# Attention decode backward on one core: two bf16 row tiles transposed as one fp32 block

## The chip, the cores and the metric

The kernel runs on one core of a Trainium2 chip. Its engines are TensorE (PE, with weight loads shown apart as PEld), VectorE (DVE), ScalarE (ACT), GpSimd (POOL) and SyncE (SP); the last two issue the DMA transfers here. The time is device microseconds of one launch. The median of three runs before the change is 1280.13 us (1279.72 to 1282.18).

## What is computed

Attention with one query row per head, forward and backward, for 64 heads (2 x 32), 8192 keys and a head size of 128, all bf16:

```python
scale = q.shape[-1] ** -0.5
scores = jnp.einsum("bhqd,bhkd->bhqk", q, k) * scale
p = _softmax(scores, axis=-1)
return jnp.einsum("bhqk,bhkd->bhqd", p, v)
```

The outputs are this result and the gradients of q, k and v for a given `grad_out`. Per head, with P the softmax row: dP = grad_out . v for every key, dS = P * (dP - sum(P * dP)), dq = scale * sum(dS * k), dk = scale * dS x q and dv = P x grad_out. K and V are read once and dK and dV are written once: 2 MB each per head, 268 MB in and 268 MB out.

## The kernel before

**Tiles.** A head's K is one tile kvt of 128 partitions x 64 rows x 128 (8192 keys, 64 on each partition), its V another. Twelve such tiles stay on chip, six heads of K and V. Later, dV is written over V and dK over K in the same tile, which is stored from there; the next load into a tile has to wait until that store has landed. Loads are issued by SyncE (L100), stores by GpSimd (L445, L89); the last head's stores go in pieces by SyncE.

**Chunks.** A tile is worked on in 4 chunks of 16 row blocks. The loop near the end counts steps g, 8 per head: in steps 0 to 3 the chunks of K are transposed, in steps 4 to 7 those of V. Everything else for a head follows at fixed steps after that, so in one step the work of up to four heads stands side by side. The order on each engine is written out by hand: every instruction of the loop goes through `pin`, which keeps program order.

**Scores.** `transpose_chunk` (L194, L196) turns 16 blocks of 128 keys x 128 into PSUM with 16 transposes, kvt as weights and a bf16 identity as the moving operand, into the tile tp (two buffers), and ScalarE copies the 128 x 2048 result to ev (two buffers). One step later `score_chunk` (L208) makes scores from it: four matmuls, each with 32 weight columns taken from qdT and 512 moving columns of ev, each into its own 32 partitions of PSUM (its own column group of the array). Among the 32 weight columns only one is not zero: qdT holds each head's q (or grad_out) column with zeros around it, so that a window shifted by the chunk's number puts the result into the chunk's own row. Over 4 chunks the tile raw collects 4 x 4 useful rows of 512. `keep_raw` (L221, VectorE) copies raw to rows, and `spread_rows` (L228) brings them back with four fp32 matmuls against a small selection matrix sel4, so that scores (or dP) stand as 128 partitions x 64.

**Softmax.** Step 5: maximum per partition on VectorE (L240). Step 6: maximum over partitions through an fp32 transpose (L244) and a reduction (L246). Step 7: spread to all partitions (L251), negated (L261), exponential on ScalarE (L271), which stands in ScalarE's queue behind the copy of step 7, then the bf16 weights E_pad (L280). Later: sums through a matmul with ones (L315), reciprocal (L324), the same for dS (L286, L338, L349, L358).

**Sums over keys.** `acc` (L372) multiplies kvt by E_pad or dS_pad, four matmuls per chunk in two column groups; `pick` (L389, L395, VectorE) and `join` (L409) reduce the result to one column. **Outer products.** `outer` (L427, VectorE) overwrites a chunk of kvt; it needs q or grad_out on all partitions, which `broadcast` (L178, L187) makes with a matmul against the identity.

**Around the change.** On TensorE, a step's order is: broadcast (steps 4 and 6), 16 transposes, joins, acc, spread_rows, max_spread, then the scores of the chunk transposed one step before. On VectorE: outer first, then the copies, maxima and sums of the step. On ScalarE: the copy of the step, in step 7 the exponential behind it. `begin` gives a head one PSUM tile sw that holds both score arrays, the broadcast and the small results. At the start q and grad_out land in qd_nat (partly by GpSimd's queue), two transposes (L154) and two copies (L155) make qdT of all heads.

Of the kernel before, what the change touches and what calls it, by code (L numbers as in the profile page):

```python
# [9 lines left out]
ALU = mybir.AluOpType  # L10
AX = mybir.AxisListType
BF16 = mybir.dt.bfloat16
F32 = mybir.dt.float32

CH = 16
QT = 4
CW = 64
NG = 2
SG = 4
SW = 32  # L20
# [6 lines left out]
def kernel(  # L27
# [11 lines left out]
    nc = tc.nc  # L39
    B, H, Sq, D = q.shape  # L40
    Sk = k.shape[2]
    P = nc.NUM_PARTITIONS
    assert Sq == 1 and D == P
    BH = B * H
# [3 lines left out]
    NCH = NT // CH  # L48
    SL = 2 * NCH
    scale = float(D) ** -0.5  # L50
# [3 lines left out]
    pin = tc.keep_in_program_order  # L54
# [65 lines left out]
        load(j, 0)  # L120
        load(j, 1)

    ident_bf = const.tile([P, P], BF16)
    masks.make_identity(nc, ident_bf[:])
    ident_f = const.tile([P, P], F32)
    masks.make_identity(nc, ident_f[:])
    ones = const.tile([P, 1], F32)
    nc.vector.memset(ones[:], 1.0)
    groups = [g * P // NG for g in range(NG)]
# [8 lines left out]
    nc.vector.memset(E_pad[:], 0.0)  # L138
    nc.vector.memset(dS_pad[:], 0.0)

    sel4 = const.tile([P, NCH, SG], F32)
    nc.vector.memset(sel4[:], 0.0)
    for g in range(SG):
        nc.vector.tensor_copy(
            out=sel4[g * SW : (g + 1) * SW, :, g],
            in_=ident_f[g * SW : (g + 1) * SW, g * SW : g * SW + NCH],
        )

    Q0 = NCH - 1
    qdT = const.tile([P, 2, Q0 + NCH * BH + SW], BF16)  # L150
    nc.vector.memset(qdT[:], 0.0)
    for w in range(2):
        tps = ps_m.tile([P, BH], BF16, tag=f"acc{w}", name="tps")
        nc.tensor.transpose(tps[:], qd_nat[:BH, w, :], ident_bf[:BH, :BH])  # L154
        nc.vector.tensor_copy(  # L155
            out=qdT[:, w, Q0 : Q0 + NCH * BH].rearrange("p (i f) -> p i f", f=NCH)[:, :, 0],
            in_=tps[:],
        )

    dqT = const.tile([P, BH], BF16)  # L160
    oT = const.tile([P, BH], BF16)
# [1 line left out]
    def begin(i):  # L163
# [7 lines left out]
        h.lsum = sw[:, 2 * NT + 2 * P : 2 * NT + 2 * P + 2]  # L171
        h.mb = sw[:, 2 * NT + 2 * P + 2 : 2 * NT + 2 * P + 3]

    def broadcast(i, w):

        h = heads[i]
        pin(
            nc.tensor.matmul(  # L178
                h.qbp,
                lhsT=qdT[:, w, Q0 + NCH * i : Q0 + NCH * i + 1].to_broadcast([P, P]),  # L180
                rhs=ident_bf[:],
                start=True,
                stop=True,
            )
        )
        h.qb[w] = small.tile([P, D], BF16, tag=f"qb{w}", name="qb")
        pin(nc.vector.tensor_copy(out=h.qb[w][:], in_=h.qbp))  # L187

    def transpose_chunk(i, c):
        w, c = divmod(c, NCH)  # L190
        src = heads[i].tile[w]
        tp = ps_tp.tile([P, CH, P], BF16, tag="tp", name="tp")
        for t in range(CH):
            pin(nc.tensor.transpose(tp[:, t, :], src[:, c * CH + t, :], ident_bf[:]))  # L194
        ev = evp.tile([P, CH, P], BF16, tag="ev", name="ev")
        pin(nc.scalar.copy(out=ev[:], in_=tp[:]))  # L196
        return ev

    def score_chunk(i, c, ev):

        h = heads[i]
        w, c = divmod(c, NCH)
        if c == 0:
            h.raw = ps_sdp.tile([P, QT * P], F32, tag="raw", name="raw")
        q0 = Q0 + NCH * i - c
        for g in range(SG):
            pin(
                nc.tensor.matmul(  # L208
                    h.raw[g * SW : (g + 1) * SW, :],
                    lhsT=qdT[:, w, q0 : q0 + SW],  # L210
                    rhs=ev[:, g * QT : (g + 1) * QT, :].rearrange("p n d -> p (n d)"),
                    start=(c == 0),
                    stop=(c == NCH - 1),
                )
            )
# [7 lines left out]
    def spread_rows(i, w):  # L223

        h = heads[i]
        for t in range(QT):
            pin(
                nc.tensor.matmul(  # L228
                    h.score[w].rearrange("p (n t) -> p n t", t=QT)[:, :, t],
                    lhsT=h.rows[:, t * P : (t + 1) * P],  # L230
                    rhs=sel4[:].rearrange("p c g -> p (c g)"),
                    start=True,
                    stop=True,
                )
            )

    def max_part(i):
        h = heads[i]
        h.mp = small.tile([P, 1], F32, tag="mp", name="mp")
        pin(nc.vector.reduce_max(out=h.mp[:], in_=h.s, axis=AX.X))  # L240

    def max_all(i):
        h = heads[i]
        pin(nc.tensor.transpose(h.mT, h.mp[:], ident_f[:]))  # L244
        h.gm = small.tile([1, 1], F32, tag="gm", name="gm")
        pin(nc.vector.reduce_max(out=h.gm[:], in_=h.mT, axis=AX.X))  # L246

    def max_spread(i):
        h = heads[i]
        pin(  # L250
            nc.tensor.matmul(  # L251
                h.mb,
                lhsT=ones[0:1, :].to_broadcast([1, P]),
                rhs=h.gm[:],
                start=True,
                stop=True,
            )
        )
        h.negm = small.tile([P, 1], F32, tag="negm", name="negm")
        pin(  # L260
            nc.vector.tensor_scalar(  # L261
                out=h.negm[:], in0=h.mb, scalar1=-scale, scalar2=None, op0=ALU.mult
            )
        )

    def expo(i):
        h = heads[i]
        h.E_f = work.tile([P, NT], F32, tag="E_f", name="E_f")
        h.ld = small.tile([P, 2], F32, tag="ld", name="ld")
        pin(  # L270
            nc.scalar.activation(  # L271
                out=h.E_f[:],
                in_=h.s,
                func=ACT.Exp,
                bias=h.negm[:],
                scale=scale,
                accum_out=h.ld[:, 0:1],
            )
        )
        pin(nc.vector.tensor_copy(out=E_pad[:, 0:NT], in_=h.E_f[:]))  # L280
# [39 lines left out]
    def normalise_p(i):  # L320
        h = heads[i]
        total(h.lsum[:, 0:1], h.ld[:, 0:1])
        h.rl = small.tile([P, 1], F32, tag="rl", name="rl")
        pin(nc.vector.reciprocal(out=h.rl[:], in_=h.lsum[:, 0:1]))  # L324
        pairs(i, 1, h.E_f, h.rl[:], "p2")
        h.rls = small.tile([P, 1], F32, tag="rls", name="rls")
        pin(
            nc.vector.tensor_scalar(
                out=h.rls[:], in0=h.rl[:], scalar1=scale, scalar2=None, op0=ALU.mult
            )  # L330
        )

    def normalise_ds(i):
        h = heads[i]
        total(h.lsum[:, 1:2], h.ld[:, 1:2])
        negdelta = small.tile([P, 1], F32, tag="negdelta", name="negdelta")
        pin(
            nc.vector.tensor_scalar(  # L338
                out=negdelta[:],
                in0=h.lsum[:, 1:2],  # L340
                scalar1=h.rl[:],
                scalar2=-1.0,
                op0=ALU.mult,
                op1=ALU.mult,
            )
        )
        dSu = work.tile([P, NT], F32, tag="dSu", name="dSu")
        pin(
            nc.vector.scalar_tensor_tensor(  # L349
                out=dSu[:],  # L350
                in0=h.dp,
                scalar=negdelta[:],
                in1=h.E_f[:],
                op0=ALU.add,
                op1=ALU.mult,
            )
        )
        pin(nc.vector.tensor_copy(out=dS_pad[:, 0:NT], in_=dSu[:]))  # L358
        pairs(i, 0, dSu, h.rls[:], "ds2")

    def acc(i, w, c):

# [42 lines left out]
    def join(i, w):  # L405

        h = heads[i]
        pin(
            nc.tensor.matmul(h.acc[w][:, 0:1], lhsT=h.sel[:], rhs=ones[:], start=True, stop=True)  # L409
        )  # L410
        pin(
            nc.vector.tensor_scalar(
                out=(oT if w else dqT)[:, i : i + 1],
                in0=h.acc[w][:, 0:1],
                scalar1=(h.rl if w else h.rls)[:],
                scalar2=None,
                op0=ALU.mult,
            )
        )
# [32 lines left out]
    last = list(range(1, NCH + 1))  # L452
    AHEAD = NTILE // 2

    prev = None
    for g in range(SL * BH + O0 + NCH + 4 - SL):
        now = [(g // SL - b, g % SL + b * SL) for b in range(4)]
# [2 lines left out]
        def at(r0):  # L460

            return next((i for i, r in now if r == r0), None)
# [37 lines left out]
        if prev is not None:  # L500
            score_chunk(*prev)
        prev = (g // SL, g % SL, ev) if ev is not None else None

        if (i := at(NCH)) is not None:
            keep_raw(i)
# [16 lines left out]

    for w, (src, dst) in enumerate(((dqT, out_1), (oT, out_0))):
        tps = ps_m.tile([BH, P], BF16, tag=f"acc{w}", name="tps")
        nc.tensor.transpose(tps[:], src[:], ident_bf[:])
        nat = evp.tile([P, CH, P], BF16, tag="ev", name="nat")
        nc.vector.tensor_copy(out=nat[:BH, 0, :], in_=tps[:])
        load_eng.dma_start(out=dst.rearrange("b h s d -> (b h s) d"), in_=nat[:BH, 0, :])
# [30 lines left out]
```

## Time and profile before

| | |
|---|---|
| median of the runs | 1280.13 us |
| profiled execution, span | 1280.2 us |
| ev copies, ScalarE, L196 | 512 x 1865 ns = 954.5 us |
| outer products, VectorE, L427 | 512 x 1216 ns = 616.8 us |
| transposes, TensorE, L194 | 8192 x 220 ns, 544.4 us busy |
| scores, TensorE, L208 | 2048 x 391 ns, 205.2 us busy |
| acc, TensorE, L372 | 2048 x 393 ns, 320 us busy |
| spread_rows weight loads, fp32, L228 | 1024 x 192 ns, 124.7 us busy |
| loads and stores | 537 MB, 421 GB/s over the span |

Busy time is the time in which at least one instruction of the row is under way. TensorE instructions are pipelined, so 8192 transposes of 220 ns each make 544 us, not 1802; what one costs in a stream is read from the distance between starts. An idle time with "<-" names what ended it. "issue" is time for which the profile shows no wait. In the chain of waits each piece is the work that the next one waited for, followed back from the end.

### The profile page before, as it was taken

How to read it: one execution, taken by the hardware profiler on the slowest of the kernel's cores; microseconds unless marked ns; L12 is line 12 of the kernel's file. 1: busy time of each engine (PE TensorE's matmuls, PEld its weight loads, DVE VectorE, ACT ScalarE, POOL GpSimd, SP SyncE). 2: the span in 40 equal slices, each digit the busy share in tenths (PEclk: the TensorE clock that was granted, in tenths of full speed). 3: DMA queues.
4: the chain of work that ended last, by engine and by line, in shares of the span. 5: the costliest groups of instructions: out<-in, count | busy, mean ns of one | idle time of the engine just before them, and what ended most of it. 6: DMA issues, size and time to landing. Idle time of an engine off the chain costs nothing.

```text
span 1280.2 us, 32473 instructions
## 1 busy us (share of the span) xinstructions
PE 1190.2 (93%) x14148; PEld 810.6 (63%) x14148; DVE 1025.8 (80%) x2256; ACT 975.3 (76%) x641; POOL 76.0 (6%) x143
## 2 busy tenths in 40 slices
PE   6999999999999999999999999999999999999994
PEld 5666666666666666666666666666666666666662
DVE  2888887888877888888888878788778888888885
ACT  6777777778777777777777777787777777777771
POOL 0000000000000000000000000000000000000000
PEclk9999999999999999999999999999999999999996
DMA  9999999999999999999999999999999999999996
GB/s 392 423 428 428 428 427 429 430 426 429 427 430 425 414 427 429 428 423 428 428 429 419 425 428 426 427 421 427 427 423 421 427 429 428 420 425 428 428 411 273
DMA packets 40155, 539.03 MB, mean 421 GB/s; under 512 B 5196, under 2 KB 5196, under 8 KB 6476
## 3 DMA queue, kind: packets, MB, share of 16 engines
q1 hardware_dynamic: 20172, 272.70, 50.1%
q0 software_dynamic: 19840, 264.25, 49.0%
q8 instruction: 110, 1.80, 0.5%
q14 instruction: 33, 0.27, 0.1%
HBM read 268.47 MB, written 268.47 MB: 419 GB/s over the span
## 4 chain that ended last, share of the span: by engine, by line
PE 59%; DVE 16%; ACT 10%; issue 10%; DMA 4%; POOL 0%; SPq 0%; ACTq 0%; POOLq 0%; DVEq 0%
PE tp L194 24%; PE acc L372 15%; ACT ev L196 9%; PE raw L208 9%; DVE kvt L427 6%; PE sw L228 4%; DVE sel L395 4%; DMA out_dram<-kvt 3%; DVE rows L221 3%; PE sw L315 3%; PE sw L178 2%; PE acc L409 2%; ACT E_f L271 1%; DVE sel L389 1%; DVE E_pad L280 1%
## 5 line engine op out<-in xcount | busy, mean ns | idle before, releaser
L196 ACT COPY ev<-tp 128x2048 bf16<-128x2048 bf16 x512 | 954.5, 1865 | 275.6 <-PE tp L194 268.9
L427 DVE TENSOR_TENSOR kvt<-qb,pair 128x2048 bf16<-128x2048 bf16 x512 | 616.8, 1216 | 0.2
L194 PE MATMUL tp<-ident_bf,kvt 128*128 128x128 bf16 x8192 | 544.4, 220 | 0.0
L194 PEld LDWEIGHTS <-kvt 128*128 128x128 bf16 x8192 | 482.4, 99 | 81.6 <-issue 80.7
L208 PE MATMUL raw<-ev,qdT 128*32 128x512 bf16 x2048 | 205.2, 391 | 1.5 <-ACT ev L196 1.5
L372 PE MATMUL acc<-kvt,E_pad 128*64 128x512 bf16 x1024 | 160.2, 393 | 24.5 <-DVE E_pad L280 24.5
L372 PE MATMUL acc<-kvt,dS_pad 128*64 128x512 bf16 x1024 | 159.8, 393 | 0.1
L228 PEld LDWEIGHTS sw<-sel,rows 128*128 128x128 f32 x1024 | 124.7, 192 | 52.4 <-DVE sel L395 25.9
L395 DVE SCALAR_TENSOR_TENSOR sel<-acc,diag,sel 128x128 f32<-128x128 f32 x384 | 134.8, 351 | 13.6
L208 PEld LDWEIGHTS <-qdT 128*32 128x32 bf16 x2048 | 53.1, 93 | 136.6 <-issue 131.8
L228 PE MATMUL sw<-sel,rows 128*128 128x16 f32 x1024 | 137.1, 266 | 0.0
L445 POOL DMA_DIRECT2D out_dram<-kvt x118 | 63.3, 536 | 1094.0 <-DVE kvt L427 555.7
L221 DVE COPY rows<-raw 128x512 f32<-128x512 f32 x128 | 88.6, 692 | 22.4 <-PE raw L208 22.4
L280 DVE CAST E_pad<-E_f 128x64 bf16<-128x64 f32 x64 | 12.5, 195 | 80.3 <-ACT E_f L271 80.3
L372 PEld LDWEIGHTS <-E_pad 128*64 128x64 bf16 x1024 | 36.1, 108 | 49.9 <-DVE E_pad L280 35.7
L178 PE MATMUL sw<-ident_bf,qdT 128*128 128x128 bf16 x128 | 28.5, 223 | 38.2 <-DVE mp L240 38.2
L246 DVE TENSOR_REDUCE gm<-sw 1x1 f32<-1x128 f32 x64 | 17.9, 279 | 55.4 <-PE sw L244 55.4
L315 PEld LDWEIGHTS sw<-ld,ones 128*128 128x128 f32 x256 | 38.1, 188 | 29.7 <-issue 15.0
L372 PEld LDWEIGHTS <-dS_pad 128*64 128x64 bf16 x1024 | 36.4, 108 | 22.3 <-DVE dS_pad L358 1.0
L315 PE MATMUL sw<-ld,ones 128*128 128x1 f32 x256 | 49.1, 261 | 0.0
L409 PE MATMUL acc<-ones,sel 128*128 128x1 f32 x256 | 43.3, 239 | 5.3 <-DVE sel L395 5.3
L389 DVE TENSOR_SCALAR sel<-acc,diag 128x128 f32<-128x128 f32 x128 | 43.8, 342 | 0.0
(49 smaller groups left out, 377.1 us busy)
## 6 DMA issues: line engine op xcount, KB each, us to landing
out_dram<-kvt POOLq DMA_DIRECT2D x118, 2048.0 KB, 40.6
kvt<-in_v_dram SPq DMA_DIRECT2D x64, 2048.0 KB, 19.1
kvt<-in_k_dram SPq DMA_DIRECT2D x63, 2048.0 KB, 19.4
out_dram<-kvt POOLq DMA_DIRECT2D x8, 2016.0 KB, 44.9
out_dram<-kvt SPq DMA_DIRECT2D x8, 512.0 KB, 10.9
kvt<-in_k_dram SPq DMA_DIRECT2D x2, 512.0 KB, 4.3
kvt<-in_k_dram SPq DMA_DIRECT2D x1, 1024.0 KB, 6.9
out_dram<-kvt POOLq DMA_DIRECT2D x8, 32.0 KB, 44.3
```

The costliest lines, as they stand in the source:

```text
L194: pin(nc.tensor.transpose(tp[:, t, :], src[:, c * CH + t, :], ident_bf[:]))
L196: pin(nc.scalar.copy(out=ev[:], in_=tp[:]))
L208: nc.tensor.matmul(h.raw[g * SW : (g + 1) * SW, :], lhsT=qdT[:, w, q0 : q0 + SW], rhs=ev[:, g * QT : (g + 1) * QT, :].rearrange("p n d -> ...
L221: pin(nc.vector.tensor_copy(out=h.rows[:], in_=h.raw[:]))
L228: nc.tensor.matmul(h.score[w].rearrange("p (n t) -> p n t", t=QT)[:, :, t], lhsT=h.rows[:, t * P : (t + 1) * P], rhs=sel4[:].rearrange("p ...
L315: nc.tensor.matmul(out, lhsT=ones[:].to_broadcast([P, P]), rhs=col, start=True, stop=True)
L372: nc.tensor.matmul(h.acc[w][g : g + CW, :], lhsT=wts[:, n0 : n0 + CW], rhs=rows[:, n0 : n0 + QT, :].rearrange("p n d -> p (n d)"), start=( ...
L389: nc.vector.tensor_scalar(out=h.sel[:], in0=block, scalar1=diag[:, 0:1], scalar2=None, op0=ALU.mult)
L395: nc.vector.scalar_tensor_tensor(out=h.sel[:], in0=block, scalar=diag[:, b : b + 1], in1=h.sel[:], op0=ALU.mult, op1=ALU.add,)
L409: nc.tensor.matmul(h.acc[w][:, 0:1], lhsT=h.sel[:], rhs=ones[:], start=True, stop=True)
L427: nc.vector.tensor_tensor(out=h.tile[w][:, n0 : n0 + CH, :].rearrange("p n (e t) -> p n e t", t=2), in0=h.qb[w][:] .rearrange("p (e t) -> ...
L445: pin(eng.dma_start(out=dst[:, b0:b1, :], in_=h.tile[w][:, b0:b1, :]))
```

## The change

Two neighbouring row blocks of kvt, 128 partitions x 256 bf16, are read as 128 x 128 fp32, each fp32 being the pair (d = 2j, d = 2j + 1) of one key row. One fp32 transpose with an fp32 identity turns them. After it, partition p holds pair j = p mod 64 of row block p div 64, and along the free side stand the 128 key partitions, each as two bf16: even d and odd d. A chunk takes 8 transposes for 16. tp and ev become 128 x 1024 fp32, as many bytes as before.

The scores are then two sums, one over even and one over odd d. `score_chunk` still makes four matmuls with 32 weight columns and 512 moving columns, but they are now (half of the chunk) x (even, odd): the moving operand is every second bf16 of ev, and the weights have two non-zero columns, one for the upper 64 partitions and one for the lower. `spread_rows` adds even and odd up, with a selection matrix that sums two column groups. The weights are no longer windows into an array of all heads: a small array qwin has zeros around two columns, and ScalarE copies a head's two columns into it (`window`), once for K and once for V. At the start there are more small transposes and copies to make q and grad_out in even and odd form (qpair), beside the plain form (qT) for the broadcast. The bf16 identity is now the upper half of the fp32 identity's elements, read with a stride. Eight one-column tiles of the softmax become columns of one tile st.

The core of the diff:

```diff
+    ident_bf = ident_f[:].bitcast(BF16).rearrange("p (n e) -> p n e", e=2)[:, :, 1]
...
+    sel4 = const.tile([P, NCH, SG // 2, 2], F32)
...
+    Q0 = 2 * NCH - 2
+    qT = const.tile([P, 2, BH], BF16)
+    qpair = const.tile([P, 2, BH, 2, 2], BF16)
+    nc.vector.memset(qpair[:], 0.0)
+    qwin = const.tile([P, 2, 2, Q0 + SW], BF16)
+    nc.vector.memset(qwin[:], 0.0)
+    qd_pair = evp.tile([P, 2, 2, 2, D // 2], BF16, tag="ev", name="qd_pair")
+    for w in range(2):
+        nc.vector.tensor_copy(
+            out=qd_pair[:BH, w],
+            in_=qd_nat[:BH, w, :]
+            .rearrange("p (j e) -> p e j", e=2)
+            .unsqueeze(2)
+            .to_broadcast([BH, 2, 2, D // 2]),
+        )
+        for e in range(2):
+            tps = ps_m.tile([P, BH], BF16, tag=f"acc{e}", name="tps")
+            nc.tensor.transpose(
+                tps[:],
+                qd_pair[:BH, w, e].rearrange("p t j -> p (t j)"),
+                ident_bf[:BH, :BH],
+            )
+            for t in range(2):
+                half = slice(t * D // 2, (t + 1) * D // 2)
+                nc.vector.tensor_copy(out=qpair[half, w, :, e, t], in_=tps[half, :])
...
+    def window(i, w):
+
+        pin(nc.scalar.copy(out=qwin[:, w, :, Q0 : Q0 + 2], in_=qpair[:, w, i]))
+
...
-        tp = ps_tp.tile([P, CH, P], BF16, tag="tp", name="tp")
-        for t in range(CH):
-            pin(nc.tensor.transpose(tp[:, t, :], src[:, c * CH + t, :], ident_bf[:]))
-        ev = evp.tile([P, CH, P], BF16, tag="ev", name="ev")
+        tp = ps_tp.tile([P, CH // 2, P], F32, tag="tp", name="tp")
+        for m in range(CH // 2):
+            n0 = c * CH + 2 * m
+            two = src[:, n0 : n0 + 2, :].rearrange("p n d -> p (n d)").bitcast(F32)
+            pin(nc.tensor.transpose(tp[:, m, :], two, ident_f[:]))
+        ev = evp.tile([P, CH // 2, P], F32, tag="ev", name="ev")
         pin(nc.scalar.copy(out=ev[:], in_=tp[:]))
...
+        q0 = Q0 - 2 * c
+        cols = (
+            ev[:]
+            .rearrange("p m s -> p (m s)")
+            .bitcast(BF16)
+            .rearrange("p (b s e) -> p b s e", b=SG // 2, e=2)
+        )
         for g in range(SG):
+            b, e = divmod(g, 2)
             pin(
                 nc.tensor.matmul(
                     h.raw[g * SW : (g + 1) * SW, :],
-                    lhsT=qdT[:, w, q0 : q0 + SW],
-                    rhs=ev[:, g * QT : (g + 1) * QT, :].rearrange("p n d -> p (n d)"),
+                    lhsT=qwin[:, w, e, q0 : q0 + SW],
+                    rhs=cols[:, b, :, e],
...
+        for m in range(QT):
             pin(
                 nc.tensor.matmul(
-                    h.score[w].rearrange("p (n t) -> p n t", t=QT)[:, :, t],
-                    lhsT=h.rows[:, t * P : (t + 1) * P],
-                    rhs=sel4[:].rearrange("p c g -> p (c g)"),
+                    h.score[w].rearrange("p (n m t) -> p n m t", m=QT, t=2)[:, :, m, :],
+                    lhsT=h.rows[:, m * P : (m + 1) * P],
+                    rhs=sel4[:].rearrange("p c b t -> p (c b t)"),
...
+        st = small.tile([P, 8], F32, tag="st", name="st")
+        h.mp, h.gm, h.negm = st[:, 0:1], st[0:1, 1:2], st[:, 2:3]
+        h.ld, h.rl, h.rls, h.negdelta = st[:, 3:5], st[:, 5:6], st[:, 6:7], st[:, 7:8]
...
+    window(0, 0)
+    window(0, 1)
...
+        if (i := at(NCH + 1)) is not None and i + 1 < BH:
+            window(i + 1, 0)
+        if (i := at(1)) is not None and i > 0:
+            window(i, 1)
```

More of the change, by code (lines that the diff above doesn't have):

```diff
@@ L121 @@
         load(j, 1)
-    ident_bf = const.tile([P, P], BF16)
-    masks.make_identity(nc, ident_bf[:])
     ident_f = const.tile([P, P], F32)
     masks.make_identity(nc, ident_f[:])
+    ident_bf = ident_f[:].bitcast(BF16).rearrange("p (n e) -> p n e", e=2)[:, :, 1]
     ones = const.tile([P, 1], F32)
@@ L139 @@
     nc.vector.memset(dS_pad[:], 0.0)
-    sel4 = const.tile([P, NCH, SG], F32)
+    sel4 = const.tile([P, NCH, SG // 2, 2], F32)
     nc.vector.memset(sel4[:], 0.0)
@@ L144 @@
         nc.vector.tensor_copy(
-            out=sel4[g * SW : (g + 1) * SW, :, g],
-            in_=ident_f[g * SW : (g + 1) * SW, g * SW : g * SW + NCH],
-        )
-    Q0 = NCH - 1
-    qdT = const.tile([P, 2, Q0 + NCH * BH + SW], BF16)
-    nc.vector.memset(qdT[:], 0.0)
+            out=sel4[g * SW : (g + 1) * SW, :, g // 2, :],
+            in_=ident_f[g * SW : (g + 1) * SW, g * SW : g * SW + 2 * NCH].rearrange(
+                "p (c t) -> p c t", t=2
+            ),
+        )
+    Q0 = 2 * NCH - 2
[23 more added lines that the diff above has]
+                nc.vector.tensor_copy(out=qpair[half, w, :, e, t], in_=tps[half, :])
     for w in range(2):
@@ L154 @@
         nc.tensor.transpose(tps[:], qd_nat[:BH, w, :], ident_bf[:BH, :BH])
[L155 to L158, printed above, removed]
+        nc.vector.tensor_copy(out=qT[:, w, :], in_=tps[:])
     dqT = const.tile([P, BH], BF16)
@@ L179, in broadcast @@
                 h.qbp,
-                lhsT=qdT[:, w, Q0 + NCH * i : Q0 + NCH * i + 1].to_broadcast([P, P]),
-                rhs=ident_bf[:],
+                lhsT=qT[:, w, i : i + 1].to_broadcast([P, P]),
+                rhs=ident_bf,
                 start=True,
@@ L204, in score_chunk @@
             h.raw = ps_sdp.tile([P, QT * P], F32, tag="raw", name="raw")
-        q0 = Q0 + NCH * i - c
+        q0 = Q0 - 2 * c
[5 more added lines that the diff above has]
+        )
         for g in range(SG):
+            b, e = divmod(g, 2)
             pin(
@@ L225, in spread_rows @@
         h = heads[i]
-        for t in range(QT):
+        for m in range(QT):
             pin(
                 nc.tensor.matmul(
-                    h.score[w].rearrange("p (n t) -> p n t", t=QT)[:, :, t],
-                    lhsT=h.rows[:, t * P : (t + 1) * P],
-                    rhs=sel4[:].rearrange("p c g -> p (c g)"),
+                    h.score[w].rearrange("p (n m t) -> p n m t", m=QT, t=2)[:, :, m, :],
+                    lhsT=h.rows[:, m * P : (m + 1) * P],
+                    rhs=sel4[:].rearrange("p c b t -> p (c b t)"),
                     start=True,
@@ L238, in max_part @@
         h = heads[i]
-        h.mp = small.tile([P, 1], F32, tag="mp", name="mp")
-        pin(nc.vector.reduce_max(out=h.mp[:], in_=h.s, axis=AX.X))
+        st = small.tile([P, 8], F32, tag="st", name="st")
+        h.mp, h.gm, h.negm = st[:, 0:1], st[0:1, 1:2], st[:, 2:3]
+        h.ld, h.rl, h.rls, h.negdelta = st[:, 3:5], st[:, 5:6], st[:, 6:7], st[:, 7:8]
+        pin(nc.vector.reduce_max(out=h.mp, in_=h.s, axis=AX.X))
     def max_all(i):
         h = heads[i]
-        pin(nc.tensor.transpose(h.mT, h.mp[:], ident_f[:]))
-        h.gm = small.tile([1, 1], F32, tag="gm", name="gm")
-        pin(nc.vector.reduce_max(out=h.gm[:], in_=h.mT, axis=AX.X))
+        pin(nc.tensor.transpose(h.mT, h.mp, ident_f[:]))
+        pin(nc.vector.reduce_max(out=h.gm, in_=h.mT, axis=AX.X))
     def max_spread(i):
@@ L253, in max_spread @@
                 lhsT=ones[0:1, :].to_broadcast([1, P]),
-                rhs=h.gm[:],
+                rhs=h.gm,
                 start=True,
@@ L258, in max_spread @@
         )
-        h.negm = small.tile([P, 1], F32, tag="negm", name="negm")
         pin(
             nc.vector.tensor_scalar(
-                out=h.negm[:], in0=h.mb, scalar1=-scale, scalar2=None, op0=ALU.mult
+                out=h.negm, in0=h.mb, scalar1=-scale, scalar2=None, op0=ALU.mult
             )
@@ L268, in expo @@
         h.E_f = work.tile([P, NT], F32, tag="E_f", name="E_f")
-        h.ld = small.tile([P, 2], F32, tag="ld", name="ld")
         pin(
@@ L274, in expo @@
                 func=ACT.Exp,
-                bias=h.negm[:],
+                bias=h.negm,
                 scale=scale,
@@ L322, in normalise_p @@
         total(h.lsum[:, 0:1], h.ld[:, 0:1])
[L323 to L326, printed above, removed]
+        pin(nc.vector.reciprocal(out=h.rl, in_=h.lsum[:, 0:1]))
+        pairs(i, 1, h.E_f, h.rl, "p2")
         pin(
             nc.vector.tensor_scalar(
-                out=h.rls[:], in0=h.rl[:], scalar1=scale, scalar2=None, op0=ALU.mult
+                out=h.rls, in0=h.rl, scalar1=scale, scalar2=None, op0=ALU.mult
             )
@@ L335, in normalise_ds @@
         total(h.lsum[:, 1:2], h.ld[:, 1:2])
-        negdelta = small.tile([P, 1], F32, tag="negdelta", name="negdelta")
         pin(
             nc.vector.tensor_scalar(
-                out=negdelta[:],
+                out=h.negdelta,
                 in0=h.lsum[:, 1:2],
-                scalar1=h.rl[:],
+                scalar1=h.rl,
                 scalar2=-1.0,
@@ L351, in normalise_ds @@
                 in0=h.dp,
-                scalar=negdelta[:],
+                scalar=h.negdelta,
                 in1=h.E_f[:],
@@ L358, in normalise_ds @@
         pin(nc.vector.tensor_copy(out=dS_pad[:, 0:NT], in_=dSu[:]))
-        pairs(i, 0, dSu, h.rls[:], "ds2")
+        pairs(i, 0, dSu, h.rls, "ds2")
     def acc(i, w, c):
@@ L414, in join @@
                 in0=h.acc[w][:, 0:1],
-                scalar1=(h.rl if w else h.rls)[:],
+                scalar1=h.rl if w else h.rls,
                 scalar2=None,
@@ L524 @@
         tps = ps_m.tile([BH, P], BF16, tag=f"acc{w}", name="tps")
-        nc.tensor.transpose(tps[:], src[:], ident_bf[:])
+        nc.tensor.transpose(tps[:], src[:], ident_bf)
         nat = evp.tile([P, CH, P], BF16, tag="ev", name="nat")
```

## The prediction

> **What bounds the kernel now.** First the page's engine and slice rows, to see which resources are near full.
>
> ```profile
> PE 1190.2 (93%) x14148; PEld 810.6 (63%) x14148; DVE 1025.8 (80%) x2256; ACT 975.3 (76%) x641; POOL 76.0 (6%) x143
> ...
> GB/s 392 423 428 428 428 427 429 430 426 429 427 430 425 414 427 429 428 423 428 428 429 419 425 428 426 427 421 427 427 423 421 427 429 428 420 425 428 428 411 273
> ```
>
> TensorE is 93% busy, and the DMA row sits at about 428 GB/s throughout: two candidates. The list of waits separates them: no TensorE row waits for a load of kvt; only stores and loads wait for compute. Second, the chain of waits in a window of two heads:
>
> ```profile
> 602.85 0.24 issue
> 603.09 1.21 DVE kvt L427
> 604.30 0.15 DVE mp L240
> 604.44 0.04 issue
> 604.49 0.22 PE sw L178
> ...
> 606.85 0.91 PE tp L194 x16
> ...
> 607.83 1.86 ACT ev L196
> 609.70 0.32 ACT E_f L271 x2
> ...
> 610.04 0.20 DVE E_pad L280
> ...
> 610.29 0.62 PE acc L372 x4
> ```
>
> One head is 19.44 us (the next "PE sw L178" of this place stands at 623.93). It has three pieces: 3.5 us in which VectorE runs from the raw scores (its copy L221 starts at 601.06) to the maximum L240, and TensorE idles 0.60 us in L178; 2.5 us in which the last transposes of a head wait for their ScalarE copy, then the exponential behind it in ScalarE's queue, then E_pad; and TensorE back to back for the rest, seven groups of 16 transposes among it. So compute sets the pace. The loads are a little ahead: the last V load is issued at 1211.5, takes some 18.2 us (the median of the last hundred microseconds), and its first chunk is transposed at 1240.8. That leaves 1240.8 - 1211.5 - 18.2 = 11 us: more than about 11 us cannot be gained before loads bind.
>
> Third, the timeline of single groups:
>
> ```profile
> 600.93 0.90 PEld L194 LDWEIGHTS <-kvt 128*128 128x128 bf16 x16 [0.23 <-issue]
> 600.94 1.07 PE L194 MATMUL tp<-ident_bf,kvt 128*128 128x128 bf16 x16
> ...
> 601.93 0.14 PEld L372 LDWEIGHTS <-dS_pad 128*64 128x64 bf16 x4
> ...
> 602.49 0.97 PEld L228 LDWEIGHTS sw<-sel,rows 128*128 128x128 f32 x8 [0.41 <-DVE sel L395]
> ...
> 603.48 0.10 PEld L208 LDWEIGHTS <-qdT 128*32 128x32 bf16 x4
> ```
>
> Sixteen bf16 transposes hold TensorE 1.00 us (600.93 to the next weight load at 601.93), (1.07 - 0.22)/15 = 0.057 us each. Eight passes with a 128x128 fp32 weight and 16 columns hold it 0.99 us (602.49 to 603.48), (0.97 - 0.19)/7 = 0.111 us each. And one fp32 transpose exists already, of one column:
>
> ```profile
> 626.02 0.27 PE L244 MATMUL sw<-ident_f,mp 128*1 128x128 f32 x1
> 626.13 1.05 PE L194 MATMUL tp<-ident_bf,kvt 128*128 128x128 bf16 x16
> ```
>
> Its 128 fp32 columns hold the array 0.11 us (0.108 in the records), and the page has 64 records for 64 heads: one pass per transpose, where L228 has 1024 for 512 calls.
>
> **Transposes (8192 bf16 to 4096 fp32).** A group of 8 needs 8 weight loads of 0.111 us and 8 streams of 0.108 us. Do load and stream overlap? L228's spacing says so: it is 0.111 us with 16 columns, and L315, with one column, has the same (two loads span 0.30, 0.30 - 0.19 = 0.11). If streaming were added, 15 columns at 0.108/128 us would show as 0.013. So I take 0.111 per transpose, hidden stream, and only the last stream exposed: 0.99 + 112 x 0.108/128 = 1.085 us per group against 1.00, +0.085. Where the operation before is full width, its stream hides part of the first load: after L178 (two groups a head) the surplus is 0.05, after L244 (one) nil, after L208 and L315 (four) 0.085. That is 0.44 us per head. The eighth group lies inside VectorE's 3.5 us and its surplus goes into L178's idle 0.60. Two joins (L409) follow a group and can hide their fp32 load behind the longer stream, -0.05 each: +0.33 us per head, 64 heads, +21 us. Bounds: below, if loads hide wholly and only 0.108 us streams count, about 0.11 a head (7 us); above, load and stream in turn, 8 x 0.219 = 1.75 against 16 x 0.057 = 0.91, +0.84 us a group; seven of them and what the idle 0.60 leaves of the eighth, 0.24, make 6.1 us a head, 390 us.
>
> The Trainium skill ("TensorE: Matmul & The Clock Gate", the section "The mechanism" of its Part 3) speaks against the change: a weight load overlaps a running matmul only when the row groups differ, and these are all full height. The trace disagrees for bf16, whose full-height loads of 0.099 us come every 0.057; by the rule taken literally the fp32 groups would cost the upper bound.
>
> **ScalarE copy (512).** The tile keeps its bytes but has 1024 fp32 elements for 2048 bf16. No row has that shape. From L196 (2048: 1865 ns) and L271 (64: 319 ns) an element costs (1865 - 319)/1984 = 0.78 ns: 1.07 us, -0.80 us a copy. If it went by bytes it would stay at 1.87. Seven of eight are hidden already; the eighth stands in the 2.5 us piece, which becomes 1.7. TensorE's own work beside it (L372 0.55, L251 0.31, L208 0.33, a group 1.0) is 2.2, so TensorE's wait for E_pad vanishes: the wait list has 24.5 us for it in all. I take -24.5; bounds 0 (by bytes) and -27. What is late next is TensorE itself.
>
> **Scores (2048, same count and widths).** The moving operand takes every second bf16. No row has a strided moving operand. Bounds: nothing (rows are as now, 0.33 us a group), or half rate, a second stream of 512 columns: L372's four in two turns take 0.62 us where L208's four in one take 0.40, so +0.22 us a group, for seven groups a head 1.54 us, +99 us (the eighth falls into L178's wait). I take nothing, nearest L208 itself: every 4-byte word read is used by one of the two column groups running side by side, and the words lie next to each other. The Trainium skill ("SBUF — State Buffer", the section "Specifications (TRN2)") states that SBUF has 16-byte lines and needs two hits per line for full rate; at 4 bytes there are four hits, so that rule gives no cost either; no run here shows it. The two broadcasts (L178), with a strided identity, change at most by 2 x 0.05 us a head, 6 us; I take 0.
>
> **Window copies on ScalarE (128 new, 128x4).** Nearest is the 0.20 us accumulator read of L271: 26 us of ScalarE in all. They stand behind a copy and need scores finished one group earlier; behind them stands the next copy, whose transposes have not ended by then (ScalarE waits 268.9 us for tp now, and its copies shrink by 410). Hidden: 0. Without that cover, 0.2 us twice a head, 26 us.
>
> **Small columns in one tile (st), sel4 and spread_rows.** Same instructions and sizes (the output of L228 only changes its stride): 0, bounds +-1 us. DMA issues and both queues, SP and POOL, are unchanged.
>
> **Start.** Before, the first transposes start at 9.08, after qd_nat lands at 8.8. Now 2 VectorE copies, 6 transposes instead of 2 and 10 small copies instead of 2 stand in front, passing to and fro through two PSUM tiles: 8 more copies of 0.16 to 0.31 (rows L144, L155) plus 4 x 0.22 and handovers, about +3.8 us. In head 0 ScalarE paces the first groups now (copies follow one another at 1.8 us from 15.26 to 22.4); at 1.07 that returns about 2.5 us. Net +1.3, bounds 0 and +4. **End.** The last head's E_pad wait (1.36 us) shrinks by 0.8.
>
> **Sum.** The profiled execution is 1280.2 us, and the median of the runs 1280.13: alike. 1280.2 + 21 - 24.5 + 1.3 - 0.8 = 1277.2.
>
> **Rivals.** (A) The sum holds: 1277, own range 1269 (21 shrinks to 7, which the 11 us of load lead then cut to 1280 - 11) to 1292 (spacing 0.115 and the full start cost: 49 streams a head x 0.004 x 64 = 12). Chance 0.50, of which faster 0.27, same 0.13, slower 0.10. (B) Transfers hide any gain: the fp32 groups are cheaper than summed and loads bind at 1269, or 1266 if the last load lands 3 us sooner than the median. For it the flat 428 GB/s, against it the 0.111 spacing. Chance 0.10, faster. (C) Slower: the strided moving read runs below full rate at L208's successor. It decides as soon as a group costs over 0.05 us more (7 x 0.05 x 64 = 22); at half rate 1277 + 99 = 1376. For it: 128 fp32 columns take 0.108 us, twice bf16's 0.057, which is what a limit on the bytes read would look like. Against it: the doubling may belong to the fp32 type, not to the read. Chance 0.20. (D) The fp32 weight load and stream get in each other's way: at 0.125 us spacing, 49 x 0.014 x 64 = +44, 1321; wholly in turn, 1277 - 21 + 390 = 1646. For it: before shows no wide load beside a wide fp32 stream. Chance 0.20, three quarters of it below 1340. (E) The change does not do what it says, transposes taking two passes as other fp32 products here: 8 more of 0.111 a group, 7 x 0.89 x 64 = +398, 1675. L244's single records speak against. Inside D's tail.
>
> About 0.2% (2.6 us) is what runs of this kernel can tell. Faster: 0.27 + 0.10 = 0.37; same 0.14; slower 0.10 + 0.20 + 0.19 = 0.49. The range reaches from B's floor up to C's price at half rate: 1266 to 1376, leaving out D's and E's tails; A's own is 1269 to 1292.
>
> **What would show it.** tp: 4096 records, spaced 0.111 us, groups of 1.08; a spacing of 0.2 is D. ev copies near 1.07 us. Score records at 0.39 us as L208 has; 0.6 is C. TensorE's wait for E_pad gone, its wait for the maximum shrinking from 0.60 a head to about 0.5. First transposes of kvt near 12.9 us. Head period 19.36. Waits of TensorE for kvt loads would show B. Wrong in another way: a new wait of TensorE behind the window copies, or a lower granted clock.

## The result

The kernel after takes 1274.12 us (median of 20 runs, 1272.57 to 1284.57); the kernel before, beside it, 1280.26 us (20 runs, 1278.15 to 1286.94). The ratio is 0.9954, 95% interval 0.9941 to 0.9967: faster by about 6 us. The profiled execution of after is a long one for it, 1278.81 us with a span of 1277.0 us, so its end is 4.7 us later than the median's; that of before (span 1280.2) lies at its median.

The page of after, first the engines and the rate of the transfers, then the groups that the change touches, then the queue of instruction fetch and the stores (packets, MB, share; KB and us from issue to landing):

```profile
PE 1193.1 (93%) x10056; PEld 785.8 (62%) x10056; DVE 1030.9 (81%) x2267; ACT 557.2 (44%) x769; POOL 75.6 (6%) x141
...
GB/s 392 425 430 428 430 429 429 429 428 429 430 428 429 423 425 429 427 422 426 429 428 423 421 430 426 428 424 430 427 430 423 426 430 429 426 422 429 430 419 254
...
q8 instruction: 79, 1.29, 0.4%
...
L222 ACT COPY ev<-tp 128x1024 f32<-128x1024 f32 x512 | 518.6, 1013 | 668.3 <-PE tp L220 662.8
...
L220 PE MATMUL tp<-ident_f,kvt 128*128 128x128 f32 x4096 | 550.5, 278 | 7.4 <-DMA kvt<-in_v_dram 6.5
L220 PEld LDWEIGHTS tp<-ident_f,kvt 128*128 128x128 f32 x4096 | 456.1, 144 | 88.4 <-issue 69.6
L241 PE MATMUL raw<-ev,qwin 128*32 128x512 bf16 x2048 | 210.0, 400 | 0.0
...
out_dram<-kvt POOLq DMA_DIRECT2D x118, 2048.0 KB, 50.8
```

ScalarE's copies fell from 1865 to 1013 ns and the engine from 76% to 44% busy. TensorE's 4096 transposes take as much busy time (550.5 us) as the 8192 did (544.4). The rate of the transfers stays at its 428 GB/s. TensorE now waits for loads of V (6.5 us), which it did not before, and a store takes 50.8 us from issue to landing for 40.6.

The chain of waits in one head of after, in the window shown of before:

```profile
611.70 0.22 PE sw L202
611.92 0.88 PE tp L220 x8
612.80 0.12 PE acc L438 x2
...
614.01 0.87 PE tp L220 x8
614.88 0.55 PE acc L401 x4
615.43 0.31 PE sw L285 x2
615.74 0.34 PE raw L241 x4
616.08 1.02 PE tp L220 x8
...
630.71 0.22 PE sw L202
```

The piece with the ScalarE copy, the exponential and E_pad is gone from it: TensorE goes from the transposes of step 7 (614.01) straight to the next acc. A head takes 630.71 - 611.70 = 19.01 us, 0.43 less than 19.44. Over 64 heads that is 27.5 us. The kernel gained 6. The end shows where the rest went. By stretches, the busy time of PE, PEld, DVE, ACT and POOL (instructions), then the granted clock, the busy share of the DMA engines and GB/s, of before:

```profile
1200.00:1240.00 40.00, 38.07 (x461) 26.12 (x462) 32.88 (x75) 31.15 (x22) 2.12 (x4) 1.00 0.99 422
1240.00:1260.00 20.00, 17.91 (x159) 10.81 (x157) 16.88 (x36) 9.60 (x7) 1.06 (x2) 0.85 0.82 349
1260.00:1280.00 20.00, 3.33 (x18) 1.42 (x14) 9.10 (x18) 0.00 (x0) 0.00 (x0) 0.59 0.61 249
```

and of after:

```profile
1200.00:1240.00 40.00, 37.11 (x312) 23.97 (x310) 33.35 (x77) 16.26 (x22) 2.13 (x4) 1.00 0.99 423
1240.00:1260.00 20.00, 8.49 (x34) 3.59 (x34) 13.50 (x28) 0.00 (x0) 0.00 (x0) 0.51 0.96 402
1260.00:1280.00 20.00, 0.00 (x0) 0.00 (x0) 0.00 (x0) 0.00 (x0) 0.00 (x0) 0.52 0.27 110
```

After 1260 before still computes (9.1 us of VectorE) with the DMA engines busy for 0.61 of the time; after has no instruction left there, only stores. The last piece of computation in the chain of waits, first of before, then of after:

```profile
1270.27 0.13 DVEq L554
```

```profile
1254.74 0.13 DVEq L589
```

It ends at 1270.4 us in before, 9.8 us ahead of the end of the span, and at 1254.9 in after, 22.1 us ahead of it. So of 15.5 us by which computation ends sooner, 12.3 were taken back by transfers that had piled up. That began earlier: heads (counted from 0) run at 19.01 us until about head 48, whose K is first used at 920.1, and at (1196.9 - 920.1)/14 = 19.77 on average from there to head 62, since in this part the lead of the loads is used up.

The rows of before held this already. A head moves 537 MB / 64 = 8.39 MB, which at 428 GB/s takes 19.6 us (an estimate), more than the 19.44 us of its computation. So the transfers were the slower of the two before the change as well, by little; the six heads that are loaded ahead hid it, and a faster computation could gain only what was left of that lead.

The first transposes of the last V, in the timeline of after:

```profile
1225.59 0.23 PE L202 MATMUL sw<-ident_f,qT 128*128 128x128 bf16 x1
1226.06 1.06 PE L220 MATMUL tp<-ident_f,kvt 128*128 128x128 f32 x8 [0.24 <-DMA kvt<-in_v_dram]
```

They come at 1226.1 against 1240.8, 14.7 us sooner, and end an idle time that a load ended.

### The profile page after: what moved, and what is told of

It is laid out like the page before. It is cut to its first block, busy times and chain, and to the rows that moved or that the text cites. A ratio compares the mean times of both kernels' runs of the same rounds, so it can differ in the third digit from the quotient of the medians.

```text
span 1277.0 us, 24554 instructions
## 1 busy us (share of the span) xinstructions
PE 1193.1 (93%) x10056; PEld 785.8 (62%) x10056; DVE 1030.9 (81%) x2267; ACT 557.2 (44%) x769; POOL 75.6 (6%) x141
## 3 DMA queue, kind: packets, MB, share of 16 engines
q8 instruction: 79, 1.29, 0.4%
## 4 chain that ended last, share of the span: by engine, by line
PE 61%; DVE 14%; DMA 9%; issue 8%; another core or an unknown queue 4%; POOL 0%; ACT 0%; SPq 0%; POOLq 0%; ACTq 0%; DVEq 0%
PE tp L220 26%; PE acc L401 15%; PE raw L241 9%; DVE kvt L456 6%; PE sw L261 4%; DVE sel L424 3%; DMA out_dram<-kvt 3%; DMA kvt<-in_k_dram 3%; DVE rows L254 3%; DMA kvt<-in_v_dram 3%; PE sw L347 2%; PE sw L202 2%; PE sw L285 1%; DVE sel L418 1%
## 5 line engine op out<-in xcount | busy, mean ns | idle before, releaser
L222 ACT COPY ev<-tp 128x1024 f32<-128x1024 f32 x512 | 518.6, 1013 | 668.3 <-PE tp L220 662.8
L220 PE MATMUL tp<-ident_f,kvt 128*128 128x128 f32 x4096 | 550.5, 278 | 7.4 <-DMA kvt<-in_v_dram 6.5
L220 PEld LDWEIGHTS tp<-ident_f,kvt 128*128 128x128 f32 x4096 | 456.1, 144 | 88.4 <-issue 69.6
L241 PE MATMUL raw<-ev,qwin 128*32 128x512 bf16 x2048 | 210.0, 400 | 0.0
L241 PEld LDWEIGHTS <-qwin 128*32 128x32 bf16 x2048 | 52.7, 93 | 136.5 <-issue 132.0
L202 PE MATMUL sw<-ident_f,qT 128*128 128x128 bf16 x128 | 28.9, 226 | 35.4 <-DVE st L275 35.4
L347 PEld LDWEIGHTS sw<-st,ones 128*128 128x128 f32 x256 | 38.1, 187 | 30.8 <-issue 15.6
L347 PE MATMUL sw<-st,ones 128*128 128x1 f32 x256 | 49.1, 261 | 0.0
L438 PEld LDWEIGHTS acc<-ones,sel 128*128 128x128 f32 x256 | 39.1, 193 | 7.2 <-DVE sel L424 7.2
L211 DVE CAST qb<-sw 128x128 bf16<-128x128 f32 x128 | 36.3, 283 | 8.0 <-PE sw L202 8.0
## 6 DMA issues: line engine op xcount, KB each, us to landing
out_dram<-kvt POOLq DMA_DIRECT2D x118, 2048.0 KB, 50.8
kvt<-in_k_dram SPq DMA_DIRECT2D x63, 2048.0 KB, 19.6
```

Source lines behind the costliest of these rows:

```text
L202: nc.tensor.matmul(h.qbp, lhsT=qT[:, w, i : i + 1].to_broadcast([P, P]), rhs=ident_bf, start=True, stop=True,)
L220: pin(nc.tensor.transpose(tp[:, m, :], two, ident_f[:]))
L241: nc.tensor.matmul(h.raw[g * SW : (g + 1) * SW, :], lhsT=qwin[:, w, e, q0 : q0 + SW], rhs=cols[:, b, :, e], start=(c == 0), stop=(c == NCH ...
L347: nc.tensor.matmul(out, lhsT=ones[:].to_broadcast([P, P]), rhs=col, start=True, stop=True)
```

## The experiments

Three theories. Theory 1: the shorter ScalarE copy is the whole gain. Theory 2: the transfers set the end of after, and computation has slack. Theory 3, formed later: what moves the end while transfers set it is that fewer instructions are fetched (TensorE executes 2 x 10056 for 2 x 14148, queue q8 moves 1.29 MB for 1.80). Ratios are to the kernel before, timed on the same chip.

**One part alone: the copy.** Before, with the same bytes copied as 1024 fp32.

```diff
-        pin(nc.scalar.copy(out=ev[:], in_=tp[:]))
+        flat = "p m d -> p (m d)"
+        pin(nc.scalar.copy(
+            out=ev[:].rearrange(flat).bitcast(F32), in_=tp[:].rearrange(flat).bitcast(F32)))
```

> The kernel before, with one edit: ScalarE's copy of tp to ev reads and writes the same bytes as 1024 fp32 elements instead of 2048 bf16. Transposes, scores and everything else stay as before. Theory 1 (the whole gain of the change is the shorter copy, by taking TensorE's wait for E_pad away; the fp32 transposes cost what the bf16 ones did): copies of 1.01 us, head period 19.0 us, the wait for E_pad gone, and a time like the changed kernel's, 1272 to 1276. Rival (the fp32 transposes themselves save TensorE time): the period stays above 19.2 us and the time above 1277.

Measured: 1280.64 us (12 runs), ratio 1.0 (0.9985 to 1.0015). The chain of waits and the list of waits (us in total, times, longest):

```profile
608.30 0.22 PE sw L178
...
611.56 0.55 PE acc L377 x4
...
627.32 0.22 PE sw L178
```

```profile
PE tp L194 <- DMA kvt<-in_v_dram: 15.1, 13, 4.9
```

The copy takes 1012 ns, E_pad no longer holds TensorE, and a head takes 19.02 us, as in after. The whole gain of computation is there (it ends at 1261.4 us, 9.0 sooner than before), and none of it reaches the end: TensorE waits for loads, and stores take 55.1 us to land. Theory 1 falls. With the bf16 transposes the transfers end at about 1280, not at 1274.

**The other parts without it.** After, with the copy over 2048 bf16.

```diff
-        pin(nc.scalar.copy(out=ev[:], in_=tp[:]))
+        pin(nc.scalar.copy(
+            out=ev[:].rearrange(flat).bitcast(BF16), in_=tp[:].rearrange(flat).bitcast(BF16)))
```

> The changed kernel, with the copy of tp to ev made over 2048 bf16 elements again. Theory 1 (the copy is the gain): copies of 1.87 us, TensorE's wait for E_pad back at 0.3 to 0.5 us a head, period 19.35 to 19.5, time 1278 to 1283. Rival (the fp32 transposes are the gain): period 19.0 to 19.1 and time at 1272 to 1276.

Measured: 1276.78 us (12 runs), ratio 0.9967 (0.9955 to 0.9978). Chain of waits:

```profile
606.38 0.22 PE sw L202
...
609.65 1.87 ACT ev L224
611.52 0.32 ACT E_f L308 x2
611.86 0.21 DVE E_pad L317
612.07 0.04 issue
612.11 0.62 PE acc L406 x4
...
625.78 0.22 PE sw L202
```

The copy and E_pad stand in the chain again, a head takes 19.40 us, and computation ends at 1270.9, where before had it (1270.4). Still the kernel is faster than before: the transfers behind it end 3.7 us later instead of 9.8, and stores land in 33.9 us. So some 0.33 of the 0.46% come without the shorter copy. The rest can't be told from nothing, since the two intervals overlap. The period is the one that Theory 1 expected, the time is not.

**The strided read.** After, with the scores read from 512 neighbouring bf16 (it sums over other elements than the reference's).

```diff
-                    rhs=cols[:, b, :, e],
+                    rhs=cols[:, g * QT * P : (g + 1) * QT * P],
```

> The changed kernel with the score matmuls reading 512 neighbouring bf16 of ev instead of every second one, so the scores are sums over other elements than the reference's. If the stride costs nothing: score records of 400 ns as in the changed kernel. If it has a small price: 391 ns as before the change. Period 18.9 to 19.0 either way, and time within 3 us of the changed kernel's.

Measured, one run: 1275.44 us, and the scores' row is

```profile
L240 PE MATMUL raw<-ev,qwin 128*32 128x512 bf16 x2048 | 205.3, 391 | 0.0
```

for 210.0 and 400 in after. The chain's group of four is 0.33 for 0.34, and a head 18.94 for 19.01 us. The step of two elements costs 9 ns a matmul, some 0.07 x 64 = 4.5 us of computation, far from half rate; at the end nothing of it can be seen in one run.

**Less computation.** After, with half of the matmuls that make the sums over keys left out.

```diff
-        for m in range(CH // QT):
+        for m in range(NG):
```

> The changed kernel with half of the sums over keys left out (two of four matmuls a chunk, line 401), which takes some 8 x 0.24 = 1.9 us a head off TensorE. Theory 2 (transfers bound the changed kernel in its last third, and the load lead is what a faster pace uses up): TensorE soon waits for loads of kvt, and the time stays at 1266 to 1275. Rival (compute still sets the pace of the changed kernel): 1274 - 64 x 1.9 = about 1152.

Measured: 1273.51 us (4 runs), ratio 0.9937 (0.9921 to 0.9954); timed again on another chip 1273.81 (5 runs), 0.9941 (0.9928 to 0.9953). From the list of waits:

```profile
POOL out_dram L474 <- DMA out_dram<-kvt: 149.9, 17, 13.7
...
PE tp L220 <- DMA kvt<-in_v_dram: 61.9, 37, 5.1
```

Computation ends at 1248.7, but the kernel as a whole ends where after does. TensorE waits for loads of V 37 times, and even the issue of stores waits for earlier stores. Its heads follow each other at 17.5 us up to head 19, and then at (1191.3 - 359.7)/42 = 19.8 from head 20 to head 62, close to the 19.6 us that the bytes of a head need. Theory 2 holds: after has reached its floor.

**Fewer bytes.** Both kernels with half of dK's rows not stored for the 55 heads that store it in one piece (57.7 MB less).

```diff
                 eng = load_eng if len(ends) > 1 else store_eng
+                if w == 0 and len(ends) == 1:
+                    b1 = NT // 2
```

Before:

> The kernel before with only the first half of dK stored, for 55 of 64 heads (1 MB each less, 58 MB of 539 in all), compute unchanged. Theory 2 (before, compute sets the pace; the change saves 0.43 us a head of it, 27 us in all, of which transfers take back some 20): this kernel stays near 1276, period 19.44, load lead growing instead of shrinking. Rival (transfers bound the kernel before too): some 135 us less, down to 1150 to 1200.

After:

> The changed kernel with the same stores left out. Theory 2: with transfers relieved the whole gain of compute shows, 64 x 0.43 less the 3.3 us of later start: 22 to 26 us under the run of the kernel before with the same stores left out, near 1252; period 19.0 to the end. Rival (the changed kernel's pace is not what the missing 21 us went to): within 10 us of that run.

Measured: 1275.06 us (7 runs) for before, 1248.30 us (4 runs, ratio 0.9714, 0.967 to 0.9759) for after. With room for the transfers the change is worth 26.8 us, close to the 0.43 us a head x 64 = 27.5 that the chains show. Before hardly gains from lighter stores: its pace was computation's. Computation ends 3.7 us ahead of the end in both (1270.5 of 1274.2, 1243.1 of 1246.8).

**Instruction fetch, first try.** After with the sums over keys made for a head's first chunk alone, and the same with 16 idle weight loads a step.

```diff
+            for _ in range(16):
+                pin(nc.tensor.ldweights(qwin[:, 0, 0, 0:SW]))
```

Without:

> The changed kernel with three quarters of the sums over keys left out (only a head's first chunk is summed, line 401): some 3 us a head less on TensorE and 3072 TensorE instructions fewer. It is the control for the next run. Transfers bound it: 1271 to 1274, TensorE waiting for loads of kvt.

With:

> The run before with 16 idle weight loads (32 columns, overwritten unused) put in front of every chunk's transposes: 8192 TensorE instructions more, of 64 bytes in the instruction fetch, 0.5 MB, for which TensorE has the time freed. Theory 3 (a kernel bound by transfers is slower the more instructions are fetched through the same DMA engines; that is why the kernel before with a short copy was no faster, and the changed kernel was): 5 to 8 us above the run before, about 1279, while TensorE still waits for loads. Rival (the number of instructions has no part in it): within 2 us of the run before. If the head period stays even and TensorE never waits for loads, the loads have become the bound themselves and the run tells nothing.

Measured: 1277.42 us (12 runs, 1272.52 to 1282.26), ratio 0.9965 (0.9942 to 0.9987), and 1279.01 us (12 runs), 0.9973 (0.9951 to 0.9995). The loads add 0.52 MB to q8 (1.10 to 1.62) and 1.6 us, which can't be told from nothing; and they are not idle enough, since computation ends at 1263.5 for 1254.7. Inconclusive. Leaving out three quarters of the sums gave no shorter time either, and not the 1271 to 1274 expected; the granted clock of the first of the two is 0.916 for after's 0.983.

**Half of the transposes.** The copy experiment with the second half of each chunk's blocks left untransposed (the scores read the first half twice).

```diff
-        for t in range(CH):
+        for t in range(CH // 2):
...
-                    rhs=ev[:, g * QT : (g + 1) * QT, :].rearrange("p n d -> p (n d)"),
+                    rhs=ev[:, g % 2 * QT : (g % 2 + 1) * QT, :].rearrange("p n d -> p (n d)"),
```

> The kernel before with the fp32 copy (run 1) and half of its transposes left out, the scores reading the same half twice: 8192 TensorE instructions fewer than run 1 (1280.6 us), about as many as the changed kernel, and 3.5 us a head less compute. Theory 3: 1273 to 1276, as the changed kernel. Rival (transfers bound run 1 at 1280 for a reason other than instructions, such as bf16 against fp32 reads on TensorE): 1279 to 1282.

Measured: 1295.24 us in the profiled execution, which was the fastest of 6 (the others 1320.54 to 1340.85), where the copy experiment took 1280.64 with more work. Stretches (the granted clock is the third number from the end), and its chain:

```profile
400.00:600.00 200.00, 185.30 (x1513) 108.13 (x1514) 153.93 (x340) 49.08 (x97) 11.02 (x20) 0.75 1.01 426
...
915.10:925.30 10.20, 10.03 (x66) 5.61 (x65) 5.81 (x14) 2.17 (x5) 0.53 (x1) 0.50 1.01 430
925.30:935.50 10.20, 9.19 (x94) 5.57 (x94) 9.85 (x22) 2.93 (x5) 0.53 (x1) 1.00 1.00 423
```

```profile
916.71 0.99 PE acc L377 x4
...
925.35 0.55 PE acc L377 x4
```

The granted clock falls to 0.75 as a mean: it changes between 0.50 and 1.00, and the same four matmuls take 0.99 us at 916.71 and 0.55 at 925.35. What this kernel saved in work it lost to the clock (its computation ends at 1289.8 of 1293.5), so it tells nothing of the transfers. The Trainium skill ("TensorE: Matmul & The Clock Gate", section "What's actually happening") has the clock passed in full or by half, according to how busy TensorE has been of late; the stretches at 0.50 and 1.00 and the two durations, 1.8 apart, agree with the first part. Why the clock falls here this run doesn't show: TensorE has less to do, but its longest wait for a load is 2.1 us, and it is busy for 185 of the 200 us shown.

**Uneven stores.** After, with dK of 14 heads instead of 8 stored as 126 + 2 partitions.

```diff
-SPREAD = range(4, 60, 7)
+SPREAD = range(4, 60, 4)
```

> The changed kernel with the split dK stores (126 + 2 partitions, line 89) for 14 heads instead of 8. The split moves work between the 16 DMA engines, and the instruction fetch, which it may balance, became smaller. Theory 3 with the fetch on few engines: fewer instructions need less balancing, so more of it is no help, 1274 to 1280. Rival (the engines were still uneven the other way): below 1272, a version better than both.

Measured: 1299.52 us (6 runs), ratio 1.0131 (1.0086 to 1.0176): 25 us slower than after, for the same bytes, and outside both expectations. The mean rate of slices 3 to 38 of the page is 421.7 GB/s for 427.3. Six more split stores cost four times what the whole change gains; by what mechanism, no trace here shows. Fewer than 8 were not tried.

**Instruction fetch, second try.** The control is the kernel with half of the sums, run again; the other adds 16 small fills on GpSimd a step.

```diff
+        for _ in range(16):
+            pin(nc.gpsimd.memset(spare[:], 0.0))
```

Control:

> The kernel after with half of the sums over keys left out, timed again as the control for the next run. All theories: 1272 to 1275 us, since the transfers set its end.

With fills:

> The control with 16 fills of one 128x1 column added on GpSimd in every step, some 8,300 instructions more on an engine that only issues stores; TensorE's own instructions stay as they are. The fetched instruction bytes of that engine should go up by about 0.5 MB. Theory 3 (the bytes and packets of instruction fetch take time from the transfers, which set the end): 4 to 6 us above the control, 1278 to 1279 us. Rival (instruction fetch has no part in the end): within 2 us of the control. Stores may be issued up to 1.6 us later, which would add at most that much.

Measured: 1273.81 us and 1453.37 us (5 runs each). GpSimd's timeline (start, us, what):

```profile
609.52 0.57 POOL L474 DMA_DIRECT2D out_dram<-kvt  x1 [0.45 <-DVE st L294]
610.07 10.00 POOL L510 MEMSET spare<- 128x1 f32 x64
620.53 0.56 POOL L474 DMA_DIRECT2D out_dram<-kvt  x1 [0.46 <-issue]
```

A fill lasts 0.099 us but the next starts 10.00 / 64 = 0.156 us after it, so 16 a step are 2.5 us, more than a step of 2.4 us. GpSimd became the bound: 620.53 - 609.52 = 11.0 us from store to store, 22.0 a head. The experiment was laid out wrong and says nothing of instruction fetch.

**What is open.** Why do transfers end at about 1274 with the new transposes and at 1280 with the old? Side by side, from the pages (q8 in MB; rate as the mean of slices 3 to 38 in GB/s; where the chain's last computation ends, and the span, us):

| kernel | q8 | rate | computation ends | span | stores land in |
|---|---|---|---|---|---|
| before | 1.80 | 426.2 | 1270.4 | 1280.2 | 40.6 |
| before, copy fp32 | 1.80 | 426.8 | 1261.4 | 1283.1 | 55.1 |
| quarter of the sums, idle loads | 1.62 | 426.4 | 1263.5 | 1281.7 | 49.0 |
| after | 1.29 | 427.3 | 1254.9 | 1277.0 | 50.8 |
| after, copy bf16 | 1.29 | 427.8 | 1270.9 | 1274.6 | 33.9 |
| after, scores contiguous | 1.29 | 428.0 | 1252.8 | 1273.7 | 52.7 |
| half of the sums | 1.16 | 428.2 | 1248.7 | 1271.2 | 67.2 |
| quarter of the sums | 1.10 | 427.5 | 1254.7 | 1276.4 | 66.4 |

The three kernels that fetch most move their data at about 1 GB/s less, 0.23% or 3 us of the span, with one profile each; after and the kernel with contiguous scores, which fetch the same, differ by 0.7 too. Three of the profiles (before with the copy in fp32, idle loads, after) are of executions 4.3 to 4.7 us above their medians. The rates fit Theory 3, but the 0.51 MB themselves would take 0.51 / 428 = 1.2 us, and the packets of q8, summed in the traces and divided over 16 engines, take 6.6 us in before and 4.7 in after, 1.9 less. The rest would have to be lost in another way, and neither try to add instructions alone came out. Against Theory 3 stands the kernel that fetches least: a quarter of the sums takes 1277.42 us, 3.3 more than after, though at a lower clock. That the fp32 transposes disturb the transfers less for another reason, such as how they read their operands, was to be told by the kernel with half of the transposes, and was not. So why the transfers of after end 4 to 6 us sooner stays open; Theory 3 is a candidate, and not shown.

## Why the prediction came out as it did

The forecast was about 1277 (sum 1277.2); 1274.1 is within its range, and the profiled execution, against which the sum was made, ended at 1277.0 of span where the sum says 1277.2. The agreement is largely chance: computation was priced some 24 us too dear (1277.2 for the 1253.5 worked out below), and the transfers, which took back 20 of them, had no term in the sum.

- **Transposes, +21: mis-sized.** Measured, next to nothing. In the chains the seven groups of a head add up to 6.53 us in after (0.88, 0.87, 1.02, 0.93, 1.02, 0.93, 0.88) and to 6.49 in the kernel that differs by the copy (0.89, 0.89, 1.00, 0.91, 1.00, 0.91, 0.89), and the two joins save 0.05 each, as the working said: -0.06 a head where it had +0.33. The timeline of one group tells why:

```profile
621.05 0.85 PEld L220 LDWEIGHTS tp<-ident_f,kvt 128*128 128x128 f32 x8 [0.24 <-issue]
621.06 1.09 PE L220 MATMUL tp<-ident_f,kvt 128*128 128x128 f32 x8
```

  Eight weight loads take 0.85 us where L228's eight fp32 loads took 0.97; one is 144 ns, not 192, and the second of the group starts 0.06 us after the first, not 0.11. The spacing itself was priced nearly right: 0.87 / 8 = 0.109 us for 0.111, which agrees with 0.108 for 128 fp32 columns, and the loads hide behind it. What failed was to put the last stream on top of L228's loads: behind the scores a group takes 1.02 us, where 1.085 was priced and 16 bf16 transposes take 1.00. With the joins, the term comes out even below the lower bound of the working (0.11 a head). Why a transpose's loads are shorter no run here shows.
- **E_pad's wait, -24.5: right in mechanism and size, for computation.** The copy is 1.01 us for 1.07 estimated, by elements and not by bytes; the period fell by 0.42 us with the copy alone and by 0.43 in after, 0.43 x 64 = 27.5, about the bound of -27.
- **The end follows the loads' lead: this step failed.** The 11 us were read from the last load alone; loads did bind, the last V is first used 14.7 us sooner. But the step took it that the end moves with it. Stores were as far behind as loads, and had no price: the stretch from that use to the end grew from 39.4 us to 50.9. Case B, with a chance of 0.10, is the mechanism that happened; its price, 1269, counted loads and not stores, and the runs put the floor near 1274. By computation alone the end would have been near 1253.5 (1280.3 - 26.8, an estimate from the two lightened kernels).
- **Scores, 0:** 400 ns for 391, +0.01 a group; nothing of half rate (case C). **Window copies, 0:** no wait of TensorE behind them. **Broadcasts, 0:** 0.22 and 0.16 as before.
- **Start, +1.3:** the first transposes come at 12.40 us (12.9 expected, 9.08 before).
- **Signs named beforehand:** 4096 records, a spacing of 0.11 (so neither D nor E) and the wait for E_pad gone: seen. Groups of 1.08: not seen; it is 1.02 at most in the chain of one head (1.09 in the timeline above counts to the end of the last record, where bf16 had 1.07). Head period 19.36: it is 19.01. The maximum's wait, 0.60 to 0.5 a head: hardly changed in the list (35.4 us for 38.2). Waits of TensorE for kvt loads: 6.5 us, which was to be the sign of B, and was.

## What to carry to other kernels

Where the transfers run at their full rate for the whole span, a gain in computation is worth only the slack up to the moment when all bytes, stores included, could have moved; look for that floor before counting a stall's removal as time: by dividing a head's bytes by the rate (19.6 us here, against 19.44 of computation), by taking bytes away (after: 1274 to 1248 us) and by taking work away (1274 stays 1274). The busy share of the DMA engines does not tell it: it read 0.9 or more in nearly every slice at 385 GB/s too, in the lightened kernels; the rate did. And the price of an operation on a new type is a sum of parts, here the first load, the spacing and the last stream: ask of each whether the row it is read from has the same part. The spacing carried over (0.111 for 0.109), the loads did not (0.192 for 0.144).

## What the runs showed of the hardware

- A 128x128 transpose of fp32 runs in one pass at 0.109 us, twice the 0.057 of bf16, and its weight load takes 0.144 us, less than the 0.192 of other fp32 loads here. Per byte the two are alike.
- ScalarE's copy from PSUM goes by elements: the same bytes take 1866 ns as 2048 bf16 and 1012 ns as 1024 fp32.
- A bf16 moving operand read at every second element costs 400 ns for 391.
- Six more stores split 126 + 2 cost 25 us (1299.5 for 1274.1), for the same bytes.
- In the kernels with less work for TensorE its mean granted clock was lower: 0.983 with all of it, 0.967 (half of the sums), 0.916 (a quarter of the sums left) and 0.805 (half of the transposes). The last ran 15 us longer than the kernel with all its transposes (1295.2 in the profiled execution for 1280.6), its clock changing between 0.50 and 1.00. The cause is not shown.
